# Feed-forward in units of 384 rows across batch borders, in a kernel of top-k attention and a gated feed-forward

## The chip, the cores and the metric

The kernel runs on one core of a Trainium2 chip. Its engines work side by side, each through its own instructions in order: TensorE (PE: matrix products; its weight loads are listed as PEld), VectorE (DVE), ScalarE (ACT), GpSimd (POOL), and SyncE (SP), which here only issues DMAs. The metric is the device time of one execution in microseconds (us), lower is better. The kernel before takes 1672.96 us, the median of 3 executions (1672.12 to 1673.5).

## The reference

```python
scores = (1 / sqrt(64)) * q @ k^T                  # per batch and head: 576 x 576
kth    = the 32nd largest score of each row
attn   = softmax over the scores >= kth, the others left out
x      = (attn @ v), heads side by side            # 4608 rows x 512
gate   = 1 / (1 + exp(-(x @ w_gate)))              # w_gate, w_val: 512 x 1536
out    = (gate * (x @ w_val)) @ w_out              # w_out: 1536 x 512
```

There are 8 batches of 576 rows, 8 heads of width 64, and 4,608 rows in all. The feed-forward part needs a precision above one pass of TensorE, so each operand is split into a high and a low part, and each product is three matmuls: high by high, high by low, low by high.

## The kernel before

**Attention steps.** A step is one batch b, one pair of heads p (4 pairs) and one tile i of 128 query rows; a batch has tiles 0 to 3 and a short one, tile 4, of 64 rows, in which the two heads share one 128-row tile. Names in the program carry b, i and p in this order: e_1_2_0 is batch 1, tile 2, pair 0. A full step handles two sets of 128 score rows (j = 0 and 1, one per head), a short one only one. A step goes through these lines:

- `scores`, lines 195 and 202: TensorE multiplies queries and keys into PSUM (tile pss), ScalarE copies them to s.
- `select`, lines 262 to 291: VectorE finds candidates (cand, line 262) and the 24 largest (tops, leads, lines 266 and 268), ScalarE marks the scores below the last of these (under, line 274), GpSimd multiplies s by this mark (u, line 277, one product over both heads), VectorE takes the 8 largest of u (below, line 281) and picks the 32nd score (pick, line 282).
- `masked`, lines 214 to 221: VectorE masks the exponentials (e, line 214, two inputs in SBUF), GpSimd prepares the sums and their inverses (lines 217 and 220).
- `turn` and `weigh`: TensorE transposes e (pt, line 301, nine transposes for a full step, five for a short one), multiplies by the values (po, lines 320 to 328), and the result is split into xh and xl (lines 343 and 344), the input of the feed-forward part. `weigh` runs once for two tiles i where they belong together: tiles 0 and 1, tiles 2 and 3, and tile 4 alone.

**Feed-forward units.** `ffn` handles a unit of rows: 256 rows (tiles 0 and 1 of a batch) or 320 rows (tiles 2 to 4), so 16 units. Each unit runs 3 groups g: four f-steps (24 matmuls each into the tiles pz, lines 377 to 379, then tanh, product and split into gh and gl, lines 382 to 385), and four e-steps (12 matmuls each into po2, lines 397 to 399, then a sum on GpSimd, line 405). That is 432 matmuls for a unit of either size. The 18 weight tiles are loaded anew for each unit (1 MB each).

**Weight tiles.** The weights come as 64-bit floats, and are split once into two 32-bit parts by `split_weight`, in two halves a tile, on every engine (lines 137 to 148; VectorE in lines 138 to 140), and stored for the later loads. Nine of the 18 tiles are split beside the first 8 attention steps, the other nine within the first unit. `split_done` gives the memory of this phase to the tiles xh and xl of batches with an odd number.

**Order.** `run` writes the steps out with a lead: queries, keys and scores some steps ahead, `masked` one step late, `turn` and `weigh` two steps late. Between steps it lets the feed-forward generator run until its work reaches a goal, which is the attention rows done less `BEHIND` = 384, with a faster start. A scheduler then fixes each engine's order when the program is built; the engines follow that order on the chip.

Of the kernel before, what the change touches and what calls it, by code (L numbers as in the profile page):

```python
# [28 lines left out]
def tile_topk_attention_then_gated_ffn(  # L29
# [125 lines left out]
    def load_keys(b, p, nm):  # L155

        ks = []
        for h in (2 * p, 2 * p + 1):
# [4 lines left out]
            nc.gpsimd.tensor_tensor(kt[D:], raw[D:], kt[D:], op=ALU.subtract)  # L163
# [79 lines left out]
    def select(J, s, col, nm):  # L243
# [33 lines left out]
        nc.gpsimd.tensor_tensor(u[:, :J], s[:, :J], under[:, :J], op=ALU.mult)  # L277
# [68 lines left out]
    def ffn(nm0, xs, t0, rows, general):  # L346
# [16 lines left out]
        n, nu = rows, 1  # L363
        units = [slice(0, n)]
        acc = [[None] * nu for _ in range(NE)]
        for g in range(NG):
            gs = [[] for _ in units]
            for f in range(FG):
                wt = load(g * FG + f)
                for j, cols in enumerate(units):  # L370
                    nm = f"{nm0}_{g}_{f}_{j}"
                    gh, gl = [pools["fg"].tile([P, U], F32R, tag=t, name=f"{t}_{nm}")[:, :n] for t in ("gh", "gl")]
                    pz = []
                    for u in range(2):
                        ps = ps_f.tile([P, U], F32, tag="f", name=f"pz_{nm}_{u}")[:, :n]
                        for d, (xh, xl) in enumerate(xs):
                            nc.tensor.matmul(ps, wt[:, u, 0, d], xh[:, cols], start=d == 0, stop=False)  # L377
                            nc.tensor.matmul(ps, wt[:, u, 0, d], xl[:, cols], start=False, stop=False)  # L378
                            nc.tensor.matmul(ps, wt[:, u, 1, d], xh[:, cols], start=False, stop=d == NP - 1)  # L379
                        pz.append(ps)  # L380
                    gf = pools["f2"].tile([P, U], F32, tag="gf", name=f"gf_{nm}")[:, :n]
                    nc.scalar.activation(gf, pz[0], AF.Tanh, scale=0.5)  # L382
                    nc.vector.scalar_tensor_tensor(gf, gf, 1.0, pz[1], op0=ALU.add, op1=ALU.mult)  # L383
                    nc.scalar.activation(gh, gf, AF.Copy)  # L384
                    nc.gpsimd.tensor_tensor(gl, gf, gh, op=ALU.subtract)  # L385
                    gs[j].append((gh, gl))
                    yield 6 * NP * n
# [22 lines left out]
    def run(general):  # L410
# [32 lines left out]
        for n in range(len(steps) + 2):  # L443
# [37 lines left out]
            if i == first:  # L481
                n = min(end * P, S) - first * P
                if b % 2 == len(bxs):
                    split_done()
# [84 lines left out]
```

## Time and profile before

| | |
|---|---|
| time, median of 3 | 1672.96 us |
| profiled execution, its own time | 1670.51 us |
| its span, first to last instruction | 1668.7 us |
| mean granted TensorE clock | 0.978 |
| busy time of PE, DVE, ACT, POOL | 1559.4, 1383.5, 1179.0, 1103.6 us |
| read from and written to HBM | 371.20 MB, 28.31 MB |

A group row of the profile reads: line, engine, operation, written tile <- read tiles, shapes, count | busy us, mean ns of one | idle us of the engine just before them and who ended it. A matmul's duration covers its way through the array, and the next one starts before it has ended; so its price is the distance from start to start, which the timeline shows. PEclk is the granted TensorE clock as a share of the full one.

### The profile page before, as it was taken

How to read it: one execution, taken by the hardware profiler on the slowest of the kernel's cores; microseconds unless marked ns; L12 is line 12 of the kernel's file. 1: busy time of each engine (PE TensorE's matmuls, PEld its weight loads, DVE VectorE, ACT ScalarE, POOL GpSimd, SP SyncE). 2: the span in 40 equal slices, each digit the busy share in tenths (PEclk: the TensorE clock that was granted, in tenths of full speed). 3: DMA queues.
4: the chain of work that ended last, by engine and by line, in shares of the span. 5: the costliest groups of instructions: out<-in, count | busy, mean ns of one | idle time of the engine just before them, and what ended most of it. 6: DMA issues, size and time to landing. Idle time of an engine off the chain costs nothing.

```text
span 1668.7 us, 37046 instructions
## 1 busy us (share of the span) xinstructions
PE 1559.4 (93%) x11666; PEld 1415.2 (85%) x11666; DVE 1383.5 (83%) x6353; ACT 1179.0 (71%) x2739; POOL 1103.6 (66%) x1331
## 2 busy tenths in 40 slices
PE   5678878899999999999999999999999999999998
PEld 2347756798999989999898989998898989999898
DVE  6999999968998889988989789988989789988310
ACT  7787878756777777766777677766777677766422
POOL 7667776866776767677666767677666767666323
PEclk8779999999999999999999999999999999999999
DMA  7556555777777677677686677677686677666686
GB/s 239 188 170 225 169 180 184 265 273 238 252 264 250 230 277 263 230 256 261 220 294 229 238 266 263 231 248 268 219 295 227 239 253 263 230 231 219 247 322 219
DMA packets 101006, 402.01 MB, mean 241 GB/s; under 512 B 11200, under 2 KB 39872, under 8 KB 65472
## 3 DMA queue, kind: packets, MB, share of 16 engines
q1 hardware_dynamic: 100800, 399.55, 68.7%
q8 instruction: 94, 1.54, 0.4%
q14 instruction: 112, 0.92, 0.2%
HBM read 371.20 MB, written 28.31 MB: 239 GB/s over the span
## 4 chain that ended last, share of the span: by engine, by line
PE 40%; DVE 24%; ACT 8%; POOL 5%; issue 3%; DMA 2%; POOLq 0%; ACTq 0%
DVE e L214 6%; PE pz L377 6%; PE pz L378 6%; PE pz L379 6%; DVE cand L262 6%; DVE below L281 4%; PE pss L195 4%; PE po L320 3%; POOL u L277 3%; PE po L397 3%; PE po L398 3%; PE po L399 3%; PE pt L301 2%; DVE pick L282 2%; ACT e L209 2%
## 5 line engine op out<-in xcount | busy, mean ns | idle before, releaser
L377 PE MATMUL pz<-xh,w 128*128 128x320 f32 (+1 forms) x1472 | 444.2, 302 | 4.4 <-DVE gf L383 2.4
L379 PE MATMUL pz<-xh,w 128*128 128x320 f32 (+1 forms) x1472 | 438.5, 298 | 0.0
L378 PE MATMUL pz<-xl,w 128*128 128x320 f32 (+1 forms) x1472 | 438.2, 298 | 0.0
L277 POOL TENSOR_TENSOR u<-s,under 128x1152 f32<-128x1152 f32 (+1 forms) x160 | 356.2, 2229 | 71.3 <-ACT under L274 54.7
L262 DVE MAX8 cand<-s 128x8 f32<-128x72 f32 x2304 | 350.5, 216 | 38.9 <-ACT s L202 38.2
L214 DVE SCALAR_TENSOR_TENSOR e<-s,kths,e 128x576 f32<-128x576 f32 x288 | 305.8, 1075 | 37.3 <-ACT e L209 37.1
L274 ACT ACTIVATE under<-s,leads 128x576 bf16<-128x576 f32 x288 | 223.3, 776 | 118.4 <-DVE leads L266 107.8
L377 PEld LDWEIGHTS pz<-xh,w 128*128 128x128 f32 x1472 | 278.7, 189 | 6.9 <-ACT gf L382 3.0
L378 PEld LDWEIGHTS pz<-xl,w 128*128 128x128 f32 x1472 | 278.9, 189 | 0.0
L379 PEld LDWEIGHTS pz<-xh,w 128*128 128x128 f32 x1472 | 278.7, 189 | 0.0
L385 POOL TENSOR_TENSOR gl<-gf,gh 128x256 fp32r<-128x256 f32 (+1 forms) x192 | 166.6, 868 | 129.0 <-ACT gh L384 126.2
L281 DVE MAX8 below<-u 128x8 f32<-128x576 f32 x288 | 205.9, 747 | 54.6 <-POOL u L277 54.4
L195 PE MATMUL pss<-k,qh 128*128 128x288 f32 (+2 forms) x672 | 204.3, 321 | 22.6 <-ACT s L202 15.5
L398 PE MATMUL po<-gl,w 128*128 128x320 f32 (+1 forms) x736 | 218.2, 301 | 0.0
L397 PE MATMUL po<-gh,w 128*128 128x320 f32 (+1 forms) x736 | 214.5, 307 | 2.6 <-ACT part L404 1.3
L399 PE MATMUL po<-gh,w 128*128 128x320 f32 (+1 forms) x736 | 215.5, 298 | 0.0
L302 ACT ACTIVATE et<-pt 128x384 f32<-128x384 f32 x384 | 181.3, 490 | 47.9 <-PE pt L301 46.8
L301 PE MATMUL pt<-ident,e 128*128 128x128 f32 x1152 | 184.2, 279 | 28.9 <-DVE e L214 24.2
L209 ACT ACTIVATE e<-s,st 128x576 f32<-128x576 f32 x288 | 209.4, 775 | 2.1 <-POOL st L270 2.1
L202 ACT ACTIVATE s<-pss 128x576 f32<-128x576 f32 x288 | 186.5, 648 | 3.3 <-PE pss L195 2.2
L195 PE MATMUL pss<-k,ql 128*128 128x288 f32 (+2 forms) x672 | 187.0, 299 | 0.3 <-POOL ql L177 0.3
L301 PEld LDWEIGHTS pt<-ident,e 128*128 128x128 f32 x1152 | 142.2, 143 | 42.5 <-DVE e L214 19.2
(102 smaller groups left out, 3543.7 us busy)
## 6 DMA issues: line engine op xcount, KB each, us to landing
w<-ws SPq DMA_DIRECT2D x276, 1024.0 KB, 5.2
v<-in_v_dram SPq DMA_DIRECT2D x64, 352.0 KB, 4.1
qraw<-in_q_dram SPq DMA_DIRECT2D x160, 128.0 KB, 3.6
kraw<-in_k_dram SPq DMA_DIRECT2D x64, 288.0 KB, 3.8
wraw<-in_w_dram SPq DMA_DIRECT2D x36, 512.0 KB, 4.0
ws<-wsplit SPq DMA_DIRECT2D x24, 512.0 KB, 4.4
ws<-wpair SPq DMA_DIRECT2D x12, 512.0 KB, 3.8
out_dram<-acc SPq DMA_DIRECT2D x32, 160.0 KB, 4.8
```

The lines of the kernel that those rows point to most:

```text
L195: nc.tensor.matmul(ps[:, half, o : o + n], x[:, h * P : (h + 1) * P], ks[h][:, k0 : k0 + n], start=t == 0, stop=t == len(todo) - 1,)
L214: nc.vector.scalar_tensor_tensor(e[:, j], s[:, j], kth[j], e[:, j], op0=ALU.is_ge, op1=ALU.mult, accum_out=st[:, 4 + j : 5 + j])
L262: nc.vector.max(cand[:, j, 8 * g : 8 * g + 8], s[:, j, g * SEG : (g + 1) * SEG])
L277: nc.gpsimd.tensor_tensor(u[:, :J], s[:, :J], under[:, :J], op=ALU.mult)
L281: nc.vector.max(below[:, j], u[:, j])
L301: nc.tensor.transpose(pt[:, c], ef[:, k0 : k0 + P], ident)
L377: nc.tensor.matmul(ps, wt[:, u, 0, d], xh[:, cols], start=d == 0, stop=False)
L378: nc.tensor.matmul(ps, wt[:, u, 0, d], xl[:, cols], start=False, stop=False)
L379: nc.tensor.matmul(ps, wt[:, u, 1, d], xh[:, cols], start=False, stop=d == NP - 1)
L397: nc.tensor.matmul(ps, wt[:, e % 2, 0, f], gh, start=f == 0, stop=False)
L398: nc.tensor.matmul(ps, wt[:, e % 2, 0, f], gl, start=False, stop=False)
L399: nc.tensor.matmul(ps, wt[:, e % 2, 1, f], gh, start=False, stop=f == FG - 1)
```

## The change

- A unit has 384 rows and may cross a batch border: 12 units in place of 16, with 432 matmuls each as before. Three units cover two batches.
- Even batches are taken in the parts tiles 0 to 2 and tiles 3 to 4, odd batches as before in tiles 0 to 1 and 2 to 4. In even batches tile 2 and tile 3 are now weighed alone, 128 rows each. Where 256 weighed rows of an odd batch reach over a unit's border (after 192 rows), xh and xl are written in two pieces.
- Twelve weight tiles (before: nine) are split beside the first 12 steps (before: 8), one a step, and all are stored and loaded again (before: three stayed in SBUF). The other six are split within unit 0. The split writes its low part in place, without a buffer of its own.
- `BEHIND` is 480, and the goal's start is steeper: 1.5 rows of feed-forward for each row of attention beyond the first 384.
- Three long GpSimd products are cut: u into halves of each head (four pieces of 288 columns for a full step, two for a short one), the keys' low part into two of 288, the weights' low part into two of 256.

```diff
-    U = 320
-    groups = [(b, *half) for b in range(B) for half in ((0, 2), (2, NT + 1))]
+    U = 3 * P
+    halves = {0: ((0, 3), (3, NT + 1)), 1: ((0, 2), (2, NT + 1))}
+    groups = [(b, *half) for b in range(B) for half in halves[b % 2]]
-    BEHIND = 384
-    HELD, LOADED = 3, 6
+    BEHIND = 480
+    LOADED, HELD = 12, 0
@@ split_weight
-            frac = pre_pools["parts"].tile([P, NP * P], F32R, tag="frac", name=f"wt_frac_{idx}_{i}")
+            frac = pair[:, 1]
...
-            nc.gpsimd.tensor_tensor(frac, frac.bitcast(F32), lead, op=ALU.mult)
+            for c in (slice(0, 2 * P), slice(2 * P, 4 * P)):
+                nc.gpsimd.tensor_tensor(frac[:, c], frac[:, c].bitcast(F32), lead[:, c], op=ALU.mult)
@@ load_keys
-            nc.gpsimd.tensor_tensor(kt[D:], raw[D:], kt[D:], op=ALU.subtract)
+            for c in (slice(0, HALF), slice(HALF, S)):
+                nc.gpsimd.tensor_tensor(kt[D:, c], raw[D:, c], kt[D:, c], op=ALU.subtract)
@@ select
-        nc.gpsimd.tensor_tensor(u[:, :J], s[:, :J], under[:, :J], op=ALU.mult)
+        for j in range(J):
+            for half in range(2):
+                c = slice(half * HALF, (half + 1) * HALF)
+                nc.gpsimd.tensor_tensor(u[:, j, c], s[:, j, c], under[:, j, c], op=ALU.mult)
@@ weigh
-        (xh, xl), c = xhl, slice(at, at + n)
-        nc.scalar.activation(xh[:, c], xf, AF.Copy)
-        nc.gpsimd.tensor_tensor(xl[:, c], xf, xh[:, c], op=ALU.subtract)
+        o = 0
+        for (xh, xl), c, k in pieces:
+            nc.scalar.activation(xh[:, c : c + k], xf[:, o : o + k], AF.Copy)
+            nc.gpsimd.tensor_tensor(xl[:, c : c + k], xf[:, o : o + k], xh[:, c : c + k], op=ALU.subtract)
+            o += k
@@ run
-                    k = m * (HELD + LOADED) // (2 * NP)
-                    for t in range(k, (m + 1) * (HELD + LOADED) // (2 * NP)):
-                        split_weight(order[t], t < HELD)
+                    early, steps0 = LOADED + HELD, 3 * NP
+                    for t in range(n * early // steps0, (n + 1) * early // steps0):
+                        split_weight(order[t], t >= LOADED)
...
-            goal = max(at - BEHIND, min(at - 2 * P, 2 * P))
-            goal *= 3 * (2 * NF * NP + NE * NF)
+            goal = max(at - BEHIND, min((at - U) * 1.5, U)) * 3 * (2 * NF * NP + NE * NF)
...
-            if o != P:
-                weigh(et, values[g, p], o, invs, xs[g][p], (i - i % 2 - first) * P, nm)
+            if len(invs) == 2 or i >= end - 1 or i == NT - 1:
+                t, left, pieces = b * S + (i + 1 - len(invs)) * P, o, []
+                while left:
+                    u, c = t // U, t % U
...
+                    k = min(left, U - c)
+                    pieces.append((xs[u, p], c, k))
+                    t, left = t + k, left - k
+                weigh(et, values[g, p], o, invs, pieces, nm)
...
-                todo.append(ffn(f"{mark}{g}", xs[g], t0, min(end * P, S) - first * P, general))
+                while (unit + 1) * U <= b * S + min(end * P, S):
+                    todo.append(ffn(f"{mark}{unit}", [xs[unit, d] for d in range(NP)], unit * U, general))
+                    unit += 1
```

The built programs show where the instructions now stand, three places of them. The first is TensorE's order at the start of unit 1 (pz_1 is its first tile, po2_0_2_3 the last of unit 0, pt a transpose, po a weighed tile, and the name behind the arrow gives the step). Before:

```order
L320 MATMUL po_1_1_2_4287<-et_1_0_2_4137,v_2_2_3521 64x256
L321 MATMUL po_1_1_2_4287<-et_1_0_2_4137,v_2_2_3521 64x256
L322 MATMUL po_1_1_2_4287<-et_1_0_2_4137,v_2_2_3521 128x256
L331 MATMUL po_1_1_2_4287<-ident_102,inv_1_0_2_3888 128x128
L331 MATMUL po_1_1_2_4287<-ident_102,inv_1_1_2_4063 128x128
L377 MATMUL pz_1_0_0_0_0_3894<-xh_1_0_1535,w_1_0_3890 128x320
L378 MATMUL pz_1_0_0_0_0_3894<-xl_1_0_1536,w_1_0_3890 128x320
L379 MATMUL pz_1_0_0_0_0_3894<-xh_1_0_1535,w_1_0_3890 128x320
```

With the change (lines are shifted there; 304 is the transpose, 379 the first matmul of an f-step):

```order
L304 MATMUL pt_1_2_0_0_4616<-ident_102,e_1_2_0_4313 128x128 x3
L400 MATMUL po2_0_2_3_3829<-gh_0_2_0_3251,wsplit_17_3777 128x384
L398 MATMUL po2_0_2_3_3829<-gh_0_2_1_3435,wsplit_17_3777 128x384
L399 MATMUL po2_0_2_3_3829<-gl_0_2_1_3436,wsplit_17_3777 128x384
L400 MATMUL po2_0_2_3_3829<-gh_0_2_1_3435,wsplit_17_3777 128x384
L398 MATMUL po2_0_2_3_3829<-gh_0_2_2_3592,wsplit_17_3777 128x384
L399 MATMUL po2_0_2_3_3829<-gl_0_2_2_3593,wsplit_17_3777 128x384
L400 MATMUL po2_0_2_3_3829<-gh_0_2_2_3592,wsplit_17_3777 128x384
L398 MATMUL po2_0_2_3_3829<-gh_0_2_3_3660,wsplit_17_3777 128x384
L399 MATMUL po2_0_2_3_3829<-gl_0_2_3_3661,wsplit_17_3777 128x384
L400 MATMUL po2_0_2_3_3829<-gh_0_2_3_3660,wsplit_17_3777 128x384
L379 MATMUL pz_1_0_0_0_4549<-xh_1_0_2112,w_1_0_4545 128x384
```

Before, unit 1 begins behind the weighing of tiles 0 and 1 of batch 1, pair 2, with 218 transposes in front of it; now behind the first transposes of tile 2 of batch 1, with 239. At the first matmul of unit 0 there are 81 transposes in front before, and 108 now; the halves of weight tiles in front of it are 17 whole ones before, and 23 now. The last weight tile (wrest_17) is finished just ahead of the start of unit 1 in both.

The second place is GpSimd's order in batch 3 around the product u of step 3_3_1. Before:

```order
L270 TENSOR_SCALAR st_3_2_1_11094<-tops_3_2_1_11092 128x2
L217 TENSOR_SCALAR st_3_4_0_10952<-st_3_4_0_10952 128x1
L277 TENSOR_TENSOR u_3_2_1_11098<-s_3_2_1_10798,under_3_2_1_11099 128x1152
L385 TENSOR_TENSOR gl_5_1_3_0_10988<-gf_5_1_3_0_11015,gh_5_1_3_0_10987 128x320
L220 COPY inv_3_4_0_11137<-st_3_4_0_10952 128x128
L177 TENSOR_TENSOR ql_3_4_2_11246<-qraw_3_4_2_11243,qh_3_4_2_11245 128x256
L344 TENSOR_TENSOR xl_6_3_10773<-xf_3_1_3_10926,xh_6_3_10772 128x256
L270 TENSOR_SCALAR st_3_3_1_11265<-tops_3_3_1_11263 128x2
L405 TENSOR_TENSOR acc_5_0_0_0_10537<-acc_5_0_0_0_10537,part_5_1_0_0_11035 128x320
L405 TENSOR_TENSOR acc_5_0_1_0_10552<-acc_5_0_1_0_10552,part_5_1_1_0_11051 128x320
L277 TENSOR_TENSOR u_3_3_1_11269<-s_3_3_1_10936,under_3_3_1_11270 128x1152
```

With the change:

```order
L280 TENSOR_TENSOR u_3_2_1_10498<-s_3_2_1_10189,under_3_2_1_10499 128x288 x2
L270 TENSOR_SCALAR st_3_3_1_10634<-tops_3_3_1_10632 128x2
L280 TENSOR_TENSOR u_3_3_1_10638<-s_3_3_1_10335,under_3_3_1_10639 128x288 x2
L217 TENSOR_SCALAR st_3_2_1_10494<-st_3_2_1_10494 128x2
L348 TENSOR_TENSOR xl_5_0_9379<-xf_3_3_0_10606,xh_5_0_9378 128x256
L220 COPY inv_3_2_1_10683<-st_3_2_1_10494 128x128
L280 TENSOR_TENSOR u_3_3_1_10638<-s_3_3_1_10335,under_3_3_1_10639 128x288 x2
```

The product was one row of 1152 columns; it is now four of 288, and the second two stand behind a sum of the step before (st, which waits for e of that step), an xl and an inverse (inv). In 116 of the 128 full steps other rows stand between the two pairs of pieces.

The third place is TensorE's order at the end of attention (po_7_4_3 is the last weighed tile of the program). Before:

```order
L328 MATMUL po_7_4_3_25209<-et_7_4_3_25199,v_15_3_24299 64x64
L331 MATMUL po_7_4_3_25209<-ident_102,inv_7_4_3_24991 128x128
L377 MATMUL pz_14_2_1_0_0_25232<-xh_14_0_22393,w_14_9_25228 128x256
L378 MATMUL pz_14_2_1_0_0_25232<-xl_14_0_22394,w_14_9_25228 128x256
L379 MATMUL pz_14_2_1_0_0_25232<-xh_14_0_22393,w_14_9_25228 128x256
```

With the change:

```order
L331 MATMUL po_7_4_3_23541<-et_7_4_3_23531,v_15_3_22775 64x64
L334 MATMUL po_7_4_3_23541<-ident_102,inv_7_4_3_23391 128x128
L398 MATMUL po2_10_2_0_23597<-gh_10_2_3_23562,w_10_16_23595 128x384
L399 MATMUL po2_10_2_0_23597<-gl_10_2_3_23563,w_10_16_23595 128x384
L400 MATMUL po2_10_2_0_23597<-gh_10_2_3_23562,w_10_16_23595 128x384
```

Behind the last weighed tile, 120 matmuls of 256 columns of unit 14 and the 432 of 320 columns of unit 15 were left; now 31 of unit 10 and the 432 of unit 11 are, all of 384 columns.

More of the change, by code (lines that the diff above doesn't have):

```diff
@@ L310, in turn, with weigh @@
             nc.scalar.activation(et[:REM, 4, :P], pt[:REM, 0], AF.Copy)
-    def weigh(et, vt, n, invs, xhl, at, nm):
+    def weigh(et, vt, n, invs, pieces, nm):
         both = ps_o.tile([P, 4 * P], F32, tag="o", name=f"po_{nm}")
@@ L361, in load @@
             return wt
-        n, nu = rows, 1
-        units = [slice(0, n)]
-        acc = [[None] * nu for _ in range(NE)]
+        acc = [None] * NE
         for g in range(NG):
-            gs = [[] for _ in units]
+            gs = []
             for f in range(FG):
                 wt = load(g * FG + f)
[L370 to L387, printed above, removed]
@@ new lines, in ffn @@
+                nm = f"{nm0}_{g}_{f}"
+                gh, gl = [pools["fg"].tile([P, U], F32R, tag=t, name=f"{t}_{nm}") for t in ("gh", "gl")]
+                pz = []
+                for u in range(2):
+                    ps = ps_f.tile([P, U], F32, tag="f", name=f"pz_{nm}_{u}")
+                    for d, (xh, xl) in enumerate(xs):
+                        nc.tensor.matmul(ps, wt[:, u, 0, d], xh, start=d == 0, stop=False)
+                        nc.tensor.matmul(ps, wt[:, u, 0, d], xl, start=False, stop=False)
+                        nc.tensor.matmul(ps, wt[:, u, 1, d], xh, start=False, stop=d == NP - 1)
+                    pz.append(ps)
@@ new lines, in ffn @@
+                nm = f"{nm0}_{g}_{e}"
+                if g == 0:
+                    acc[e] = pools["f4"].tile([P, U], F32, tag="acc", name=f"acc_{nm}")
+                ps = ps_f.tile([P, U], F32, tag="f", name=f"po2_{nm}")
+                for f, (gh, gl) in enumerate(gs):
+                    nc.tensor.matmul(ps, wt[:, e % 2, 0, f], gh, start=f == 0, stop=False)
+                    nc.tensor.matmul(ps, wt[:, e % 2, 0, f], gl, start=False, stop=False)
+                    nc.tensor.matmul(ps, wt[:, e % 2, 1, f], gh, start=False, stop=f == FG - 1)
@@ new lines, in ffn @@
+                if g == 0:
+                    nc.scalar.activation(acc[e], ps, AF.Copy, scale=0.5)
+                else:
+                    part = pools["f2"].tile([P, U], F32, tag="gf", name=f"part_{nm}")
+                    nc.scalar.activation(part, ps, AF.Copy, scale=0.5)
+                    nc.gpsimd.tensor_tensor(acc[e], acc[e], part, op=ALU.add)
+                if g == NG - 1:
+                    nc.sync.dma_start(out[e * P : (e + 1) * P, t0 : t0 + U], acc[e])
+                yield 3 * FG * U
@@ L410, in run @@
     def run(general):
         steps = [(g, p, i) for g, (_, first, end) in enumerate(groups) for p in range(NP) for i in range(first, end)]
-        keys, values, qs, staged, xs = {}, {}, {}, {}, [[] for _ in groups]
+        keys, values, qs, staged, xs = {}, {}, {}, {}, {}
         mark = "g" if general else ""
@@ L439, in run @@
             begin(m)
-        todo, work, at, col = [], 0, 0, 0
+        todo, work, at, col, unit = [], 0, 0, 0, 0
         parts, done = {}, {}
@@ L480, in run @@
             e, inv = done.pop(n - 2)
[L481 to L484, printed above, removed]
-                xs[g].append(
-                    [bxs[b % 2].tile([P, n], F32R, tag=f"{t}{first}", name=f"{t}{mark}_{g}_{p}") for t in ("xh", "xl")]
-                )
-            if i % 2 == 0:
+            if i == first or (i - first) % 2 == 0 or i == NT:
                 et, o, invs = b2.tile([P, 9, 2 * P], F32, tag="et", name=f"et_{nm}"), 0, []
```

43 lines of the change are left out of this document (17 added, 26 removed).

## Prediction

> **What bounds the kernel now.** I read the page first, then busy time by stage, then TensorE's waits, then single groups.
>
> ```profile
> span 1668.7 us, 37046 instructions
> PE   5678878899999999999999999999999999999998
> DVE  6999999968998889988989789988989789988310
> PEclk8779999999999999999999999999999999999999
> 0.00:310.00 310.00, 231.28 (x1333) 170.26 (x1334) 291.20 (x1226) 254.91 (x547) 214.84 (x239) 0.89 0.59 196
> 310.00:1556.00 1246.00, 1222.45 (x9558) 1142.76 (x9557) 1081.49 (x5100) 895.23 (x2122) 858.15 (x1053) 1.00 0.71 249
> 1556.00:1668.70 112.70, 105.64 (x779) 102.18 (x777) 10.81 (x29) 28.84 (x72) 30.65 (x40) 0.98 0.75 273
> ```
>
> The rows by stage give PE, PEld, DVE, ACT and POOL busy. There are three stages. Up to 310 us VectorE is busy for 291.2 of 310 us while TensorE is at a lowered clock (0.89) with holes. From 310 to 1556 us TensorE is busy for 1222 of 1246 us, VectorE for 87%, GpSimd for 69%. Behind that only feed-forward is left. The same view for line 214 (e) alone counts the steps:
>
> ```profile
> 0.00:310.00 310.00, 48.80 (x96) 0.89 0.59 196
> 310.00:1556.00 1246.00, 258.93 (x480) 1.00 0.71 249
> ```
>
> Each half of a step has two instructions there (the product and its accumulator read), so the second stage holds 480 / 4 = 120 full steps, 1081.5 / 120 = 9.0 us of VectorE each. The first holds 24; beside them 291.2 - 24 x 9.0 = 75 us go to the 18 weight tiles, 4.2 us a tile.
>
> Busy time of TensorE hides holes, since matmuls overlap. Its waits in the time from 310 us on are the check:
>
> ```profile
> PE pss L195 <- ACT s L202: 10.4, 17, 1.1
> PE pt L301 <- ACT et L302: 4.5, 5, 0.9
> PE pz L377 <- ACT gf L382: 2.0, 4, 0.5
> ```
>
> They are small. So VectorE sets the pace up to 310 us and TensorE behind it; what counts is when unit 1 starts, and how much TensorE has to do from there.
>
> ```profile
> 310.37 0.39 PE L377 MATMUL pz<-xh,w 128*128 128x320 f32 x1
> ```
>
> This is unit 1's first matmul: 310.4 us, and 1668.7 - 310.4 = 1358.3 us are left behind it.
>
> **Part 1: fewer, wider matmuls.** The price of one is its distance to the next.
>
> ```profile
> L377 PE MATMUL pz<-xh,w 128*128 128x320 f32 x768 | 240.6, 313 | 3.3 <-ACT gf L382 2.0 <-DVE gf L383 1.3
> L377 PE MATMUL pz<-xh,w 128*128 128x256 f32 x704 | 203.5, 289 | 1.1 <-DVE gf L383 1.1
> 1602.04 0.31 PE L377 MATMUL pz<-xh,w 128*128 128x320 f32 x1
> 1602.48 0.31 PE L377 MATMUL pz<-xh,w 128*128 128x320 f32 x1
> ...
> 1399.94 0.28 PE L377 MATMUL pz<-xh,w 128*128 128x256 f32 x1
> 1401.02 0.28 PE L377 MATMUL pz<-xh,w 128*128 128x256 f32 x1
> ...
> 307.00 0.40 PE L146 MATMUL wrest<-wsplit,minus 128*128 128x512 f32 x1
> 307.24 0.41 PE L147 MATMUL wrest<-wt_frac,plus 128*128 128x512 f32 x1
> ```
>
> With 320 columns, three matmuls take 0.44 us, 0.1467 each; with 256, nine take 1.08, 0.120 each. The line through both is 0.417 ns a column and a fixed 13.3 ns, so 384 columns come to 0.1733. The row of 512 columns gives 0.24 from its two starts, and drawn from 320 to 512 the line gives 0.177 at 384; I keep that as the upper end, and take 0.1733, since 384 is nearer to the two rows that a long run of equal matmuls shows. In the 1358.3 us behind unit 1's start, 8 units of 320 and 7 of 256 rows are left: 8 x 432 x 0.1467 + 7 x 432 x 0.120 = 507.0 + 362.9 = 869.9 us. After the change 11 units: 11 x 432 x 0.1733 = 823.5 us (840 at the upper end). That is **-46.4 us**: about 21 of it from the fixed part, the rest because unit 0 takes 128 more rows ahead of this point, where TensorE has holes.
>
> On the fixed part the Trainium skill says otherwise: "TensorE: Matmul & The Clock Gate", section "Wait — 56ns, not 53.3ns?", gives N / 2.4 GHz plus about 2.5 ns. By that the 1,728 matmuls less of the whole kernel would be worth 4 us, not 23, and most of what a matmul costs above its columns would be no fixed part; the first rival below is that case.
>
> **Part 2: when unit 1 starts.** In the orders shown ahead, unit 1's first matmul has 218 transposes in front before, 239 now: 21 / 9 = 2.3 steps later in attention, with all 18 weight tiles split in both. VectorE sets the pace here, so 2.3 x 9.0 = **+21 us**. Unit 0 brings 128 more rows, 432 x (0.1733 - 0.120) = 23 us of TensorE into a stretch that is no longer by as much, and its first matmul has 108 transposes in front, not 81; VectorE's time covers nearly all of it, and I add **+4** (the whole lateness is a rival below). The steps moved ahead leave the rest: 1358.3 - 869.9 = 488 us of attention and stalls for the 1,312 - 218 = 1,094 transposes that were left, 0.446 each, 21 fewer: **-9 us**.
>
> **Part 3: GpSimd's products in pieces.** The first question is what they do to VectorE.
>
> ```profile
> L214 DVE SCALAR_TENSOR_TENSOR e<-s,kths,e x288: 790/814/2927, 27.0 to 1554.2; 128x576 f32<-128x576 f32 x144
> L282 DVE SCALAR_TENSOR_TENSOR pick<-wanted,sums,below x288: 198/222/2404, 25.5 to 1553.8; 128x8 f32<-128x8 f32 x144
> L214 DVE SCALAR_TENSOR_TENSOR e<-s,kths,e 128x576 f32<-128x576 f32 x288 | 305.8, 1075 | 37.3 <-ACT e L209 37.1
> L282 DVE SCALAR_TENSOR_TENSOR pick<-wanted,sums,below 128x8 f32<-128x8 f32 x288 | 125.6, 451 | 0.3
> 137.22 2.32 DVE L214 SCALAR_TENSOR_TENSOR e<-s,kths,e 128x576 f32<-128x576 f32 x1
> ...
> 136.55 2.38 POOL L277 TENSOR_TENSOR u<-s,under 128x1152 f32<-128x1152 f32 x1
> DVE below L281 <- POOL u L277: 51.9, 47, 2.9
> ```
>
> The first two rows give minimum, median and maximum: the mask takes 814 ns as a rule and up to 2927, the pick 222 and up to 2404, though their sizes never change. At 137.22 us a mask of 2.32 us ends (139.54) just behind GpSimd's product (138.93): it waited for that product to end. Over the kernel this costs (1075 - 814) x 288 + (451 - 222) x 288 = 75 + 66 = 141 us of VectorE.
>
> ```profile
> L277 POOL TENSOR_TENSOR u<-s,under 128x1152 f32<-128x1152 f32 x128 | 312.5, 2445 | 57.0 <-ACT under L274 45.2 <-DMA w<-ws 2.6 <-ACT et L302 2.6
> L277 POOL TENSOR_TENSOR u<-s,under 128x576 f32<-128x576 f32 x32 | 43.8, 1367 | 14.3 <-ACT under L274 9.4 <-PE pss L195 4.0 <-DMA w<-ws 0.6
> L385 POOL TENSOR_TENSOR gl<-gf,gh 128x256 fp32r<-128x256 f32 x96 | 79.1, 824 | 43.2 <-ACT gh L384 41.2 <-PE pt L301 0.6
> L163 POOL TENSOR_TENSOR k<-kraw,k 64x576 fp32r<-64x576 f32 x64 | 97.1, 1518 | 23.3 <-issue 8.0 <-PE pss L195 3.9 <-DMA kraw<-in_k_dram 3.4
> ```
>
> From 2445 and 1367 ns the product costs 1.87 ns a column and 289 ns fixed, so a piece of 288 columns about 0.83 us, which the 256 columns of gl (0.824) support. A full step's product grows from 2.45 to 3.31 us; with keys and weights at the same fixed 0.3 us a cut, GpSimd gets 128 x 0.87 + 32 x 0.29 + 64 x 0.3 + 36 x 0.3 = 150 us more, and at most 48 x 0.824 = 40 us less by 48 fewer gl. Its 1104 us become 1214 to 1254, 74 to 77% of the new span, and are hidden behind TensorE; the cover ends where VectorE comes to wait for u more than now (the last row of the fence above, 51.9 us). What a waiting VectorE instruction pays goes with the square of the product's length: by these rows the sum over all products falls by about a third (a full step's u from 6.0 to 2.8), worth 47 us of VectorE. A fifth of it lies ahead of 310 us, where VectorE sets the pace: **-10 us** (bounds 0 and -20). The rest lies where TensorE bounds, and keeps VectorE below the 87% of now in spite of the shorter time.
>
> **Part 4: tiles weighed alone.** Sixteen pairs of 128 and 128 rows in place of 256.
>
> ```profile
> 1502.32 0.38 PE L320 MATMUL po<-et,v 128*64 128x256 f32 x1
> 1502.54 0.38 PE L320 MATMUL po<-et,v 128*64 128x256 f32 x1
> ...
> 1509.76 0.22 PE L325 MATMUL po<-et,v 128*64 128x64 f32 x1
> 1509.82 0.22 PE L325 MATMUL po<-et,v 128*64 128x64 f32 x1
> ```
>
> 0.22 us with 256 columns and 0.06 with 64, so about 0.11 with 128: no loss but the start and end of each group. I take 0.4 us each, **+6 us** (between 0 and 18, a second full price of some 1.1 us).
>
> The third place of the orders costs nothing: 552 narrower matmuls (120 x 0.120 + 432 x 0.1467 = 78 us) are left behind the last weighed tile before, 463 (80 us) now.
>
> **The sum.** Unit 1 starts at 310.4 + 21 + 4 - 10 = 325. Behind it 1358.3 - 46.4 - 9 + 6 = 1309. Span 1634; the profiled execution's own time (1670.51) lies 1.8 above its span, and the median of the runs shown (1672.96) 2.4 above that: **1638 us**, 2.1% faster.
>
> **Rivals.**
> - *The excess of a matmul is a share, not a fixed part.* For it speaks the row of 512 columns (0.177 at 384), against it the two long runs. 11 x 432 x 0.0037 = 17 us more: 1655. Chance 0.10.
> - *VectorE's relief reaches TensorE too.* If TensorE's waits on ScalarE and VectorE behind 310 us (the rows above and smaller ones, some 20 us) mostly go and the start gains the full 20: 1638 - 10 - 16 = 1612. Chance 0.12.
>
> The next two rest on these rows, unit 0's first matmul and the spread (minimum, median, maximum) of the product u:
>
> ```profile
> 133.80 0.70 PE L377 MATMUL pz<-xh,wsplit 128*128 128x256 f32 x1
> ...
> L277 POOL TENSOR_TENSOR u<-s,under x160: 1278/2396/3032, 21.4 to 1550.5; 128x1152 f32<-128x1152 f32 x128, 128x576 f32<-128x576 f32 x32
> ```
>
> - *Slower: the later first unit.* If TensorE and not VectorE sets the pace of unit 0, its lateness is passed on whole: 27 transposes more (3 steps, 27 us) and three more tiles split ahead of it, at 4.2 us each, make 39 us, and unit 0 takes the 177 us of now (from 133.8 to 310.4) plus 23. Unit 1 then starts at about 133.8 + 39 + 177 + 23 = 373, the span is 373 + 1309 = 1682, the time 1686. It decides where TensorE is busy throughout from its first matmul to unit 1's, which the 231 of 310 us speak against. Chance 0.07.
>
> - *Slower: the pieces come too late.* The second two pieces stand behind a sum and an inverse that wait for VectorE. If below of the second head waits 0.87 us longer in each of the 109 full steps left, and TensorE behind it, that is 95 us: 1733. It decides once the waits of VectorE for u pass the 52 us of now by as much. Against it: the first head's pieces are done 1.66 us after their start, before 2.45. Chance 0.05. The product itself is held up too, up to 3.03 us against a median of 2.40. The Trainium skill ("SBUF — State Buffer", section "Who interferes with whom") gives the ports to whichever comes first, for its whole instruction, and the mask of 2.32 us above agrees; each of the three more starts of a step can then find a mask of VectorE ahead of it, which is how this rival would come about.
>
> - *No change.* Half of the later first unit (+24) with two thirds of the dearer matmul (+11): 1673. Chance 0.04.
>
> **Numbers.** The forecast has 0.62. What a measurement here can tell from no change is 0.2%, 3.3 us. Faster: 0.62 + 0.10 + 0.12 = 0.84; within: 0.04; slower: 0.07 + 0.05 = 0.12, together 1. The range goes from the second rival (1612) to the first with the upper ends of parts 4 (+12) and 2 (+1): 1668.
>
> **What would show it.** Right: a start-to-start of 0.173 us at 384 columns; unit 1 at 315 to 335 us; from there TensorE without waits above those of now; the mask's mean nearer to its median; GpSimd near 1214 us busy. Wrong: unit 1 behind 350 us; VectorE waiting for u well above 52 us; TensorE waiting for gl or e.

## The result, and the profile after

The changed kernel takes 1634.38 us (median of 5 runs, 1633.64 to 1634.91), the kernel before 1672.21 us beside it (5 runs, 1669.97 to 1673.5). The ratio is 0.9779, with a 95% interval of 0.9767 to 0.9790: 2.2% faster, where 2.1% (1638 us) was forecast. The profiled execution took 1634.38 us.

From the page of the changed kernel, the span; behind it its busy time by stage, cut at the same times as before (columns: the stretch, its length, then PE, PEld, DVE, ACT, POOL busy with their counts, granted clock, DMA share, GB/s):

```profile
span 1632.5 us, 34064 instructions
...
0.00:310.00 310.00, 251.61 (x1370) 190.63 (x1371) 283.97 (x1224) 255.62 (x545) 251.75 (x368) 0.88 0.62 206
310.00:1556.00 1246.00, 1230.69 (x8463) 1144.17 (x8462) 1080.10 (x5088) 902.12 (x2064) 913.15 (x1412) 1.00 0.58 202
1556.00:1632.50 76.50, 69.46 (x397) 68.40 (x396) 6.09 (x11) 16.45 (x34) 19.41 (x20) 0.98 0.60 218
```

The picture is the one of before: VectorE nearly full ahead of 310 us (284 of 310), TensorE behind it (1230.7 of 1246, before 1222). What is shorter is the last stage, 76.5 us in place of 112.7: attention ends sooner.

TensorE's timeline (start, duration, operation) at unit 0's first matmul, at unit 1's, and in a run of equal matmuls of the last unit:

```profile
164.92 0.76 PE L379 MATMUL pz<-xh,w 128*128 128x384 f32 x1
...
325.29 0.33 PE L379 MATMUL pz<-xh,w 128*128 128x384 f32 x1
...
326.33 0.33 PE L379 MATMUL pz<-xh,w 128*128 128x384 f32 x1
...
1600.09 0.33 PE L379 MATMUL pz<-xh,w 128*128 128x384 f32 x1
...
1602.35 0.33 PE L380 MATMUL pz<-xl,w 128*128 128x384 f32 x1
```

Unit 1 starts at 325.3 us, forecast 325, and 1632.5 - 325.3 = 1307.2 us lie behind it, forecast 1309. Six matmuls take 326.33 - 325.29 = 1.04 us, 0.1733 each; thirteen at the end 2.26 us, 0.174 each.

The groups of line, engine and shape that the pieces concern (count | busy us, mean ns | idle before it and its releaser), the spreads of mask and pick (minimum, median, maximum in ns), and the waits of TensorE behind 331 us and of VectorE for u behind 310:

```profile
L280 POOL TENSOR_TENSOR u<-s,under 128x288 f32<-128x288 f32 x576 | 443.8, 792 | 110.6 <-ACT under L274 102.1 <-PE pt L304 1.1 <-ACT xh L347 0.5
L214 DVE SCALAR_TENSOR_TENSOR e<-s,kths,e 128x576 f32<-128x576 f32 x288 | 289.3, 1005 | 10.7 <-ACT e L209 7.9
L387 POOL TENSOR_TENSOR gl<-gf,gh 128x384 fp32r<-128x384 f32 x144 | 150.0, 1042 | 99.0 <-ACT gh L386 95.2
L285 DVE SCALAR_TENSOR_TENSOR pick<-wanted,sums,below 128x8 f32<-128x8 f32 x288 | 125.9, 437 | 3.2 <-DVE leads L266 0.3 <-issue 0.2
L137 DVE SCALAR_TENSOR_TENSOR wraw<-wraw,wt_lead 128x512 uint32<-128x512 uint32 x36 | 32.0, 888 | 0.3
...
L214 DVE SCALAR_TENSOR_TENSOR e<-s,kths,e x288: 792/876/1547, 28.5 to 1516.0; 128x576 f32<-128x576 f32 x144
L285 DVE SCALAR_TENSOR_TENSOR pick<-wanted,sums,below x288: 199/327/1080, 26.9 to 1513.5; 128x8 f32<-128x8 f32 x144
...
PE pss L195 <- ACT s L202: 3.9, 9, 1.1
PE pt L304 <- ACT et L305: 3.8, 3, 1.9
PE po L398 <- ACT part L405: 1.7, 2, 0.9
...
PE po L399 <- POOL gl L387: 0.8, 2, 0.4
PE po L328 <- DVE xf L340: 0.7, 1, 0.7
...
DVE below L284 <- POOL u L280: 49.6, 81, 2.8
```

The worst mask falls from 2927 to 1547 ns, the worst pick from 2404 to 1080, and the means only from 1075 to 1005 and from 451 to 437: fewer long holds, more short ones. So both figures of the sum came out, unit 1's start and what lies behind it. The relief under them did not: mask and pick cost VectorE (70 + 14 ns) x 288 = 24 us less, where the pieces were to spare it 47. A sum that comes out says little about its terms, which can be wrong against each other; the experiments take them apart.

### The profile page after: what moved, and what is told of

It is laid out like the page before. It is cut to its first block, busy times and chain, and to the rows that moved or that the text cites. A ratio compares the mean times of both kernels' runs of the same rounds, so it can differ in the third digit from the quotient of the medians.

```text
span 1632.5 us, 34064 instructions
## 1 busy us (share of the span) xinstructions
PE 1551.8 (95%) x10226; PEld 1403.2 (86%) x10226; DVE 1370.2 (84%) x6321; ACT 1174.2 (72%) x2643; POOL 1184.3 (73%) x1799
## 4 chain that ended last, share of the span: by engine, by line
PE 34%; DVE 7%; POOL 7%; ACT 3%; issue 2%; POOLq 0%; ACTq 0%; DVEq 0%
PE pz L381 5%; PE pz L380 5%; PE pz L379 5%; PE pss L195 3%; PE po L398 3%; POOL u L280 2%; PE pt L304 2%; PE po L400 2%; PE po L399 2%; PE po L323 2%; DVE cand L262 2%; DVE e L214 2%; DVE below L284 1%; POOL k L163 1%; PE po L325 1%
## 5 line engine op out<-in xcount | busy, mean ns | idle before, releaser
L280 POOL TENSOR_TENSOR u<-s,under 128x288 f32<-128x288 f32 x576 | 443.8, 792 | 110.6 <-ACT under L274 102.1
L379 PE MATMUL pz<-xh,w 128*128 128x384 f32 x1120 | 383.4, 344 | 1.0 <-ACT xh L347 1.0
L380 PE MATMUL pz<-xl,w 128*128 128x384 f32 x1120 | 380.0, 339 | 1.2 <-POOL xl L348 1.2
L381 PE MATMUL pz<-xh,w 128*128 128x384 f32 x1120 | 380.1, 339 | 0.0
L214 DVE SCALAR_TENSOR_TENSOR e<-s,kths,e 128x576 f32<-128x576 f32 x288 | 289.3, 1005 | 10.7 <-ACT e L209 7.9
L284 DVE MAX8 below<-u 128x8 f32<-128x576 f32 x288 | 216.3, 751 | 58.8 <-POOL u L280 57.8
L387 POOL TENSOR_TENSOR gl<-gf,gh 128x384 fp32r<-128x384 f32 x144 | 150.0, 1042 | 99.0 <-ACT gh L386 95.2
L380 PEld LDWEIGHTS pz<-xl,w 128*128 128x128 f32 x1120 | 211.1, 188 | 2.0 <-POOL xl L348 2.0
L379 PEld LDWEIGHTS pz<-xh,w 128*128 128x128 f32 x1120 | 210.3, 188 | 2.1 <-ACT xh L347 1.3
L381 PEld LDWEIGHTS pz<-xh,w 128*128 128x128 f32 x1120 | 210.7, 188 | 0.0
L398 PE MATMUL po<-gh,w 128*128 128x384 f32 x560 | 189.7, 351 | 2.7 <-ACT part L405 1.7
L399 PE MATMUL po<-gl,w 128*128 128x384 f32 x560 | 190.8, 341 | 0.8 <-POOL gl L387 0.8
L400 PE MATMUL po<-gh,w 128*128 128x384 f32 x560 | 189.9, 340 | 0.0
```

The costliest lines, as they stand in the source:

```text
L214: nc.vector.scalar_tensor_tensor(e[:, j], s[:, j], kth[j], e[:, j], op0=ALU.is_ge, op1=ALU.mult, accum_out=st[:, 4 + j : 5 + j])
L280: nc.gpsimd.tensor_tensor(u[:, j, c], s[:, j, c], under[:, j, c], op=ALU.mult)
L284: nc.vector.max(below[:, j], u[:, j])
L379: nc.tensor.matmul(ps, wt[:, u, 0, d], xh, start=d == 0, stop=False)
L380: nc.tensor.matmul(ps, wt[:, u, 0, d], xl, start=False, stop=False)
L381: nc.tensor.matmul(ps, wt[:, u, 1, d], xh, start=False, stop=d == NP - 1)
```

## The experiments

Each was timed in 4 or 5 runs beside the kernel before; the ratios are to that.

**Does a matmul cost a fixed part beside its columns?**

```diff
+                    for c in (slice(0, U // 2), slice(U // 2, U)):
                         for d, (xh, xl) in enumerate(xs):
-                            nc.tensor.matmul(ps, wt[:, u, 0, d], xh, ...)
+                            nc.tensor.matmul(ps[:, c], wt[:, u, 0, d], xh[:, c], ...)
```

(so for all six lines of feed-forward matmuls: twice as many, of 192 columns)

> The change with each feed-forward matmul of 384 columns issued as two of 192 (5,184 become 10,368; rows, units, loads and sums stay). Theory: each matmul has a fixed 13.3 ns above its columns, so 192 columns cost 0.0933 us, 10,368 of them 967.7 us in place of 898.6: +69 us where TensorE sets the pace, about 1700 us. Rival (what a matmul costs above its columns is a share of them): 192 columns cost 0.087 us and the time stays within 10 us of 1634. By the Trainium skill's 2.5 ns a matmul it would be +13 us, 1647.

Measured: 1852.84 us, ratio 1.1078 (1.1061 to 1.1095). From its TensorE timeline:

```profile
899.89 0.27 PE L400 MATMUL po<-gh,w 128*128 128x192 f32 x1
...
900.33 0.27 PE L401 MATMUL po<-gl,w 128*128 128x192 f32 x1
```

Three more matmuls start between the two: 0.44 / 4 = 0.11 us each, where the line through 256 and 320 columns gives 0.0933. So the line holds from 256 to 384 columns (above) and not at 192: 10,368 matmuls at 0.111 are 1151 us in place of 5,184 x 0.1733 = 898, and account for more than the 218 us by which this kernel is slower. My 1700 us and the rival's 1634 both missed. The fixed part holds at 384, but a matmul of 192 columns costs what the line gives for 232 (0.11 = 0.0133 + 0.000417 x 232); what sets its 0.11 us no run here shows.

**The two halves of the change apart.** The changed kernel with u, keys and weights whole again, and the kernel before with nothing but the pieces:

```diff
...
-        for j in range(J):
-            for half in range(2):
-                c = slice(half * HALF, (half + 1) * HALF)
-                nc.gpsimd.tensor_tensor(u[:, j, c], s[:, j, c], under[:, j, c], op=ALU.mult)
+        nc.gpsimd.tensor_tensor(u[:, :J], s[:, :J], under[:, :J], op=ALU.mult)
```

> The change with the three GpSimd products whole again (u over both heads, keys, weights). Theory: the pieces only relieve VectorE where it sets the pace, up to unit 1, by some 10 us; unit 1 starts at 335 us and the time is about 1644. Rival one: the pieces are worth nothing or cost something, 1634 or less. Rival two: they carry much of the gain, since TensorE waits less too: 1655 or more.

> The kernel before with nothing but the pieces (u, keys and weights cut as in the change; units, parts, splits and lags as before). Theory: the same 10 us ahead of unit 1, about 1662. Rival one: nothing, 1672. Rival two: 20 us or more, 1652 or less, if the pieces also shorten TensorE's stage.

Measured: without the pieces 1664.22 us, 0.9953 (0.994 to 0.9967); the pieces alone 1642.68 us, 0.9816 (0.9802 to 0.9829). So the pieces are worth 30 us, with either kind of unit (1672 to 1643, 1664 to 1634), and units, parts, lag and split together 8. I had 10 and 24; in both runs it is the second rival (the pieces carry much of the gain) whose figure came. Unit 0's and unit 1's first matmul in the timeline without the pieces, and unit 1's with the pieces alone:

```profile
185.60 0.76 PE L374 MATMUL pz<-xh,w 128*128 128x384 f32 x1
...
346.36 0.34 PE L374 MATMUL pz<-xh,w 128*128 128x384 f32 x1
```

```profile
307.94 0.45 PE L382 MATMUL pz<-xh,w 128*128 128x320 f32 x1 [0.71 <-ACT part L409]
```

| profiled execution | unit 1 starts | behind it | span |
|---|---|---|---|
| before | 310.4 | 1358.3 | 1668.7 |
| new units, no pieces | 346.4 | 1315.0 | 1661.4 |
| old units, pieces | 307.9 | 1335.0 | 1642.9 |
| the change | 325.3 | 1307.2 | 1632.5 |

The units by themselves start 36 us later and save 43 behind; the pieces then take 21 off the start and 8 off the rest. The scheduler orders each program anew: without the pieces 242 transposes stand ahead of unit 1, with them 239 (counted from the matmuls' records), a third of a step, so 3 us of the 36 and of the 21 are that. The busy time up to unit 1's start without the pieces, cut at unit 0's first matmul:

```profile
0.00:186.00 186.00, 118.14 (x512) 76.40 (x512) 171.24 (x695) 148.76 (x308) 125.53 (x138) 0.80 0.56 193
186.00:346.40 160.40, 148.76 (x941) 128.52 (x940) 147.50 (x602) 123.69 (x275) 111.36 (x122) 0.97 0.59 206
```

VectorE is busy there for 171.2 + 147.5 = 318.7 us, in the change for 298.6 (its rows are shown further down). So nearly all of the 21 us at the start is VectorE's: 12 of them lie in the three operations of the weight split (2362 ns together without the pieces, 2028 with them, 36 times), 4 in mask and pick.

On the old units the pieces' gain is nearly all behind the start (23 us; 6 of these are 13 transposes more that stand ahead of it, at 0.446). The rest shows as TensorE's waits, which for the pieces alone have all but gone: the view lists 5.3 us behind the start, and 22.7 there in the kernel before. The largest of the 5.3, and two rows of the run without pieces:

```profile
PE po L402 <- ACT acc L406: 1.6, 5, 0.3
PE po L402 <- DMA w<-ws: 0.8, 2, 0.4
PE pz L382 <- ACT part L409: 0.7, 1, 0.7
PE po L402 <- DVE st L220: 0.7, 1, 0.7
...
PE po L394 <- POOL gl L382: 3.5, 5, 1.3
...
PE po L323 <- DVE xf L335: 3.4, 3, 2.2
```

With the new units the pieces take TensorE's waits behind the start from 19.6 to 13.3 us, and most of that is in these two rows, which stand at 0.8 and 0.7 in the change: one waits for GpSimd, the other for VectorE.

**Does VectorE alone set the start?** The changed kernel without the three VectorE operations of the weight split:

```diff
-            nc.vector.tensor_scalar(lead_u, lead_u, 3, None, op0=ALU.logical_shift_left)
-            nc.vector.scalar_tensor_tensor(top, top, 0x80000000, lead_u, ...)
-            nc.vector.tensor_scalar(lead_u, top, 0xFF800000, None, op0=ALU.bitwise_and)
```

> The change without the three VectorE operations of the weight split (so the split weights are not the reference's). Theory: VectorE sets the pace up to unit 1, so most of its 75 us of splitting come off unit 1's start (325 us), limited by ScalarE at 256 us busy in the first 310: unit 1 at 260 to 285, time 1570 to 1595. Rival (TensorE with the first matmul of unit 0 late sets the pace there): unit 1 earlier by 20 us at most, time 1614 or more.

Measured: 1623.41 us, 0.9698 (0.9682 to 0.9714). It takes away 36 x (888 + 583 + 557 ns) = 73 us of VectorE and brings 11. Its busy time in the stretches up to unit 1's start at 310.6 us (columns as above):

```profile
0.00:60.00 60.00, 36.95 (x133) 21.81 (x134) 33.27 (x161) 52.50 (x105) 50.02 (x87) 0.91 0.85 279
60.00:118.00 58.00, 41.26 (x176) 25.36 (x174) 37.08 (x182) 51.03 (x107) 37.91 (x60) 0.82 0.73 248
...
180.00:250.00 70.00, 67.94 (x463) 63.27 (x457) 55.65 (x251) 46.85 (x108) 50.92 (x81) 0.98 0.53 180
250.00:310.00 60.00, 58.71 (x342) 47.73 (x341) 46.89 (x210) 57.34 (x125) 49.51 (x75) 1.00 0.75 249
```

With VectorE free (33 of 60, 37 of 58), ScalarE is at 88% up to 118 us, TensorE waits 23.7 us for raw weights (tile wraw) by its view of waits, and from 180 us on TensorE is busy for 126.6 of 130 us. Unit 0 comes 46 us sooner (118.5 for 164.9) and unit 1 only 15, and that with two steps of attention less in front of it (221 transposes in place of 239). So my expectation fell, and the rival's figures came: VectorE is the first of several limits that lie close together. The changed kernel itself shows it, cut at unit 0's first matmul, and the kernel before beside it:

```profile
0.00:165.00 165.00, 113.57 (x472) 70.75 (x472) 151.15 (x640) 141.02 (x290) 135.66 (x198) 0.80 0.64 208
165.00:325.00 160.00, 151.28 (x979) 131.31 (x978) 147.48 (x642) 127.92 (x287) 129.57 (x191) 0.98 0.62 213
```

```profile
133.80:310.40 176.60, 147.25 (x1006) 118.36 (x1004) 172.32 (x726) 146.18 (x326) 125.42 (x138) 0.96 0.58 194
```

In unit 0's stretch VectorE was busy for 98% before, TensorE for 83%; now it is 92% and 95%.

**Why do the pieces help: shorter holds, or a first head that is done sooner?** u's four pieces in another order (the first head is whole only after the third); u in two, a head each, keys and weights whole; only u in four, keys and weights whole:

```diff
-        for j in range(J):
-            for half in range(2):
+        for half in range(2):
+            for j in range(J):
```

```diff
...
-            for half in range(2):
-                c = slice(half * HALF, (half + 1) * HALF)
-                nc.gpsimd.tensor_tensor(u[:, j, c], s[:, j, c], under[:, j, c], op=ALU.mult)
+            nc.gpsimd.tensor_tensor(u[:, j], s[:, j], under[:, j], op=ALU.mult)
```

> The change with the four pieces of u in another order: first half of both heads, then second half of both. The pieces are as short, but the first head is whole only after the third piece (2.4 us) and not after the second (1.6). Theory A (what helps is that GpSimd holds VectorE's two-input instructions for a shorter time): 1634, within 4 us. Theory B (what helps is that the first head's product is ready early): much of the 30 us of the run without pieces is lost, 1645 or more.

> The change with u in two products of 576 columns, one a head, and the products of keys and weights whole. The first head is ready about as early (1.3 us), GpSimd has half of the cuts, and a product holds VectorE for up to 1.3 us. Theory A (length of the hold): between the two, 1644 to 1656. Theory B (first head early): 1640 or less.

> The change with only u in pieces, the products of keys and weights whole. Tells which cuts carry the 30 us. If u does: 1636 within 4 us. If keys and weights, which lie mostly ahead of unit 1's start, do: 1650 or more.

Measured: 1635.18 us, 0.9782 (0.9769 to 0.9795); 1649.34 us, 0.9863 (0.9847 to 0.9878); 1643.17 us, 0.9828 (0.9815 to 0.9842). The order makes no difference, so it is not the early head. u whole, in two, in four: 1664, 1649, 1643; cutting keys and weights as well brings the last 9 (the run with only u in four lies between its two expectations). The mask's spread and its row with u whole and with u in two, each beside its product:

```profile
L212 DVE SCALAR_TENSOR_TENSOR e<-s,kths,e x288: 790/808/2908, 26.5 to 1550.3; 128x576 f32<-128x576 f32 x144
L212 DVE SCALAR_TENSOR_TENSOR e<-s,kths,e 128x576 f32<-128x576 f32 x288 | 277.4, 981 | 5.3 <-ACT e L207 5.2
L275 POOL TENSOR_TENSOR u<-s,under 128x1152 f32<-128x1152 f32 x128 | 307.5, 2403 | 67.3 <-ACT under L272 59.0 <-PE pss L193 2.0 <-PE wrest L145 1.3
```

```profile
L212 DVE SCALAR_TENSOR_TENSOR e<-s,kths,e x288: 791/819/1999, 25.8 to 1544.6; 128x576 f32<-128x576 f32 x144
L212 DVE SCALAR_TENSOR_TENSOR e<-s,kths,e 128x576 f32<-128x576 f32 x288 | 303.0, 1053 | 12.0 <-ACT e L207 9.4 <-ACT s L200 0.5
L276 POOL TENSOR_TENSOR u<-s,under 128x576 f32<-128x576 f32 x288 | 380.5, 1323 | 141.3 <-ACT under L272 131.6 <-PE po L321 1.9 <-ACT xh L343 1.4
```

The longest hold (maximum less minimum) is 2.12 us beside a product of 2.40, 1.21 beside 1.32, and 0.76 in the change beside pieces of 0.79 (the longest left, gl and the sum into acc, take 1.04 and 1.06): it goes with the product. The Trainium skill ("SBUF — State Buffer", section "Who interferes with whom") calls the port pair that VectorE and GpSimd share "an exclusive lock", for which a VectorE instruction with two SBUF inputs contends; the trace agrees.

The holds in all do not go with the time. With u whole, in two, in four, and in the change the mask's mean is 981, 1053, 1028 and 1005 ns and VectorE is busy for 1377.9, 1398.5, 1376.4 and 1370.2 us, while the time falls from run to run. So what the pieces shorten is the longest hold; that this is how they help is shown ahead of unit 1's start, where VectorE's busy time falls by 20 us and the start by 21, and is argued behind it. A rival was not tested there: small pieces also let GpSimd's own rows (gl, xl, the sums) start sooner than behind a whole u, and the wait for gl above says that a part of the gain is that. The order of the pieces does not tell the two apart.

**The pace of the weight split.** Nine tiles beside the first eight steps in place of twelve beside twelve:

```diff
-    LOADED, HELD = 12, 0
+    LOADED, HELD = 9, 0
...
-                    early, steps0 = LOADED + HELD, 3 * NP
+                    early, steps0 = LOADED + HELD, 2 * NP
...
```

> The change with the old pace of splitting: nine tiles beside the first 8 steps, the other nine within unit 0. VectorE's work up to unit 1 is the same. Theory (engine work up to unit 1 sets its start, not where the splits stand): within 6 us of 1634. Rival (splitting beside the first steps carries part of the gain, since unit 0's last group otherwise waits for nine tiles in a row): 1645 or more.

Measured: 1636.19 us, 0.979 (0.9776 to 0.9803), which the measurement cannot tell from the change. Unit 0 comes at 120.9 us in place of 164.9, unit 1 at 335.9 in place of 325.3, with a step more of attention ahead of it (57 products e in place of 54).

**The lag of feed-forward.**

```diff
-    BEHIND = 480
+    BEHIND = 384
```

> The changed kernel with the lag of feed-forward behind attention (BEHIND) back from 480 to 384 rows. Theory (start and TensorE's content set the time): the lag only says which of two ready kinds of work TensorE takes; behind unit 1's start TensorE is busy in both, so the time stays at 1634, within 4 us. Rival (the longer lag is needed with 384-row units, since with 384 rows attention runs too short of feed-forward work at some point): the time goes up by 6 us or more, with TensorE waiting for xh or xl of unit rows just finished.

Measured: 1658.51 us, 0.992 (0.9906 to 0.9934). The rival was right: without the longer lag the wider units lose 24 us, and are 16 us slower than the old ones with the same pieces. Unit 1's start is the same (325.2); all of it lies behind. There are 16 stretches of more than 4 us there in which no feed-forward matmul runs, 124 us together; the changed kernel has 2, of 12 us (counted from the matmuls' records). One of them, by TensorE's groups, then all engines in it, and TensorE's waits behind 326 us:

```profile
L324 PE MATMUL po<-et,v 128*64 128x128 f32 x16 | 3.1, 353 | 0.0
L323 PE MATMUL po<-et,v 128*64 128x128 f32 x16 | 3.1, 354 | 2.3 <-DVE xf L340 2.3
...
L379 PE MATMUL pz<-xh,w 128*128 128x384 f32 x1 | 0.4, 423 | 0.0
...
948.80:960.80 12.00, 9.37 (x77) 8.09 (x75) 11.70 (x50) 10.00 (x23) 10.34 (x18) 0.86 0.22 56
...
PE pss L195 <- ACT s L202: 12.6, 18, 2.8
PE pz L380 <- POOL xl L348: 3.7, 8, 1.2
```

The one pz is the stretch's last instruction. Without feed-forward beside it, attention goes at the pace of VectorE (11.70 of 12 us), and TensorE rests. A unit is ready only when a part of a batch is done, at 384, 832, 1152, 1536, 1984 rows of attention, at or up to 64 rows behind its own rows; a lag of 384 has then just used up the unit before. TensorE's waits come to 28 us, in the change to 13; where the rest of the 24 us lies within the stretches I did not take apart.

**Can it be bettered?** gl and acc, the feed-forward products that grew to 384 columns, in two of 192; u in eight of 144; a lag of 512:

```diff
-                nc.gpsimd.tensor_tensor(gl, gf, gh, op=ALU.subtract)
+                for c in (slice(0, U // 2), slice(U // 2, U)):
+                    nc.gpsimd.tensor_tensor(gl[:, c], gf[:, c], gh[:, c], op=ALU.subtract)
...
```

```diff
-            for half in range(2):
-                c = slice(half * HALF, (half + 1) * HALF)
+            for half in range(4):
+                c = slice(half * HALF // 2, (half + 1) * HALF // 2)
```

> The changed kernel with GpSimd's two 384-column feed-forward operations (gl and the addition to acc) also cut, each into two of 192 columns. In the changed kernel these two hold VectorE's mask and pick for 27 + 16 = 43 us in all, up from 19 us before the change. Theory (shorter holds of VectorE help wherever they are cut): this clash falls to about 20 us, GpSimd's busy time goes up by 220 x 0.25 = 55 to 70 us, and since these operations lie nearly all behind unit 1's start, where the pieces brought 9 us for 18 to 34 us of holds, the time falls by 3 to 8 us, to 1626 to 1631. Rival (behind unit 1's start TensorE bounds, and a later gl makes the next group of matmuls wait): 1634 to 1640.

> The changed kernel with u in eight pieces of 144 columns a step in place of four of 288. By the rows of 288 and 576 columns (0.74 and 1.29 us) a piece of 144 takes some 0.46 us, so GpSimd gets about 144 x 0.8 = 115 us more and comes to 1300 us busy, 80% of the span. Theory (only the hold's length counts): the mask's and pick's clash with u falls from 39 us to about 20, a quarter of it ahead of unit 1, and the time falls by 5 to 10 us to 1624 to 1629. Rival (GpSimd's own lateness now costs: below and the halves of k stand behind more of its work): VectorE's waits for u rise above 80 us and the time is 1636 to 1650.

> The changed kernel with the lag of feed-forward behind attention at 512 rows in place of 480. Units become ready at 384, 832, 1152, 1536, 1984 rows of attention, so unit 1, 4, 7 are ready 64 rows after the 384 x (unit + 1) rows that they hold; a lag of 384 then leaves TensorE without feed-forward work, from 448 on there is always some. Theory (the lag only has to cover these 64 rows and the step's grain): nothing more is gained above 480, the time is 1634 within 4 us. Rival (the lag is slack in proportion, 24 us for 96 rows, so a quarter of a microsecond a row): 8 us less, 1626. Second rival (a later start of unit 1's bulk costs a step, 5 us): 1639.

Measured: 1637.53 us, 0.9794 (0.978 to 0.9807); 1637.89 us, 0.9798 (0.9785 to 0.9811); 1636.75 us, 0.9788 (0.9774 to 0.9801). None beats the change. With u in eight, the mask, u, VectorE's wait for u, and TensorE's for gl behind 327 us:

```profile
L214 DVE SCALAR_TENSOR_TENSOR e<-s,kths,e 128x576 f32<-128x576 f32 x288 | 277.1, 963 | 10.0 <-ACT e L209 7.8 <-PE pss L195 1.0
L280 POOL TENSOR_TENSOR u<-s,under 128x144 f32<-128x144 f32 x1152 | 568.6, 526 | 89.8 <-ACT under L274 79.1 <-PE pz L381 1.9 <-PE pt L309 1.7
...
DVE below L284 <- POOL u L280: 78.1, 110, 2.8
...
PE po L399 <- POOL gl L387: 7.7, 7, 2.3
```

The holds go on shrinking (the mask by 42 ns, 12 us over 288), but GpSimd has 125 us more to do for u (568.6 for 443.8), VectorE waits 78 us for it over the whole run (57.8 in the change) and TensorE now waits for gl. From four pieces to eight the trade is about even. With gl and acc cut it is the same trade: VectorE is busy for 1357.8 us, 12 less than in the change, and waits 81.5 us for u, 24 more. A lag of 512 gains nothing over 480: the lag has only to cover what the parts leave late.

## Why the prediction was right, step by step

- **What bounds the kernel.** Behind unit 1's start TensorE: right; 12 us less of VectorE there (gl and acc cut) brought nothing, though its longer waits for u stand against them. Ahead of it "VectorE sets the pace": right up to unit 0's first matmul, too simple behind it, where TensorE and VectorE are both above 90% after the change, and where taking 73 us from VectorE moved unit 1 by 15.
- **Part 1** (-46 us for fewer, wider matmuls). The price, 0.1733, is exact, so the first rival (1655) is out. The figure of the Trainium skill ("TensorE: Matmul & The Clock Gate", section "Wait — 56ns, not 53.3ns?"), columns / 2.4 GHz plus 2.5 ns, gives 0.1625 at 384 columns, and the measured number decides. Of the 46 us the fixed part is 4 units x 432 x 13.3 ns = 23, not 21. But the term was not paid out in full. With parts 1, 2 and 4 I had 1358.3 - 49 = 1309 us behind the start; without the pieces it was 1315.0. And it needs the lag of 480, which I left without a price: at 384 it is 1657.4 - 325.2 = 1332 us. The step that was missing is "does TensorE always have a unit at hand?"; its answer at the old lag costs 24 us.
- **Part 2** (+21 and +4). Mis-sized: without the pieces unit 1 starts 36 us later, not 25. With 242 transposes in front of it, the price of the term gives +24 for the steps; so the +4 for what unit 0 adds should have been about +12. Unit 0 is late by 185.6 - 133.8 = 52 us there, and 16 of these are made good before unit 1. That lies between my term and the rival of the later first unit, which took the lateness at 39 and passed all of it on. That rival's bound, TensorE busy throughout, came closer than I allowed: 148.8 of the 160.4 us without the pieces.
- **Part 3** (-10). Mis-sized: -30. At the start it was -21 (346.4 to 325.3). I took a fifth of a third of the holds of mask and pick, and had that third at 47 us; beside the run without pieces the two fell by (981 + 491 - 1005 - 437) x 288 ns = 9 us, and their busy time ahead of the start by 4. The three VectorE operations of the weight split were left out; they fell by 12 us there, 7 of these (1086 to 888 ns, 36 times) in the one with two inputs. Behind the start I set nothing, since TensorE bounds; it was -8 with the new units and -23 with the old, where TensorE's waits went: the mechanism of my second rival, which I held apart with a chance of 0.12. GpSimd's part was right: a piece 0.79 us (0.83 forecast), 1184 us busy (1214 forecast), VectorE's wait for u behind 310 us 49.6 (51.9 before), so that the rival of late pieces did not come about.
- **Part 4** (+6 for tiles weighed alone) was not measured by itself.
- **The sum.** The start came out at 325.3 because +11 in part 2 and -11 in part 3 cancel, and the rest at 1307 because the units' 6 too little and the pieces' 8 too much do. The time was right, and two terms of it were wrong by 16 and 20 us. That they cancel is luck: nothing in the prediction ties the one to the other.

## What to carry to other kernels

Where VectorE and GpSimd both work on SBUF with two inputs, look at minimum, median and maximum of a VectorE instruction of fixed size: if the maximum goes with the length of a GpSimd product, cut that product, until its fixed cost (here 0.2 to 0.3 us a piece) eats what the shorter holds give. The mean does not tell: it rose here from 981 to 1005 ns while the time fell. When units of work grow, ask at which rows they become ready and whether the lag still covers that; the gain of the wider matmuls was there only with both. And a forecast that meets the total proves none of its terms: undo one part and do one part alone before believing the sum.

## What was not expected of the hardware

- Matmuls of 192 columns start 0.11 us apart, no sooner than some 230 columns would by the line of the wider ones; halving 384 columns costs 2 x 0.111 - 0.173 = 0.049 us a pair.
- In the stretch from 948.8 to 960.8 us with the lag of 384, in which TensorE was busy for 9.37 of 12 us, the granted clock was 0.86. A stretch without feed-forward does not lower it by itself: of the 16 it was 1.00 in 14, and the changed kernel has 0.86 from 1067 to 1079 us, with TensorE busy for 10.3 of 12.
- A piece of u of 144 columns takes 526 ns in the mean and one of 288 takes 792, which would leave 0.26 us that do not depend on the columns. The medians, 462 and 737 ns, leave 0.19; the rest comes of single pieces that take longer, up to 1084 ns.
